# Where the hidden activations are squared, copied and split, in a three-stage attention and two-layer MLP kernel in a hand-ordered schedule

## The chip, the cores and the metric

One core of a Trainium2 chip. The kernel runs as one program on that core. The metric is the device time of one execution in microseconds (us). The median of three timed runs of the kernel before is 681.76 us (680.63 to 685.14).

## The reference, cut to what matters

Three stages follow one another. An attention over 1536 tokens (2 batches, 8 heads, head size 64) gives x of 1536 rows and 512 columns. Then come two blocks of the same shape, each with 512 inputs, 2048 hidden units and 512 outputs. They differ in the activation:

```python
h = x @ w_in
r = np.maximum(h, 0.0)
g = r * r
x = g @ w_out                      # first block

h = x @ w_in
g = np.where(h >= 1, h, np.where(h <= -1, 0.0, (h + 1) ** 2 / 4))
out = g @ w_out                    # second block
```

Inputs and outputs are fp32, the weights fp64. A matmul in one pass isn't exact enough, so each operand is held as a rounded high part and a low part (the rest), and three products (high with high, low with high, high with low) are summed.

## The kernel before, in words

The order of the work is a table of words, PLAN (lines 61 to 162), that is read from left to right: each word is a step (letters), its number and, last, an engine (a for ScalarE, v for VectorE, g for GpSimd). Steps are issued in that order, and each engine runs its own instructions strictly in the order in which they were issued; semaphores hold an instruction until its inputs are there and its output buffer is free. So the table sets, for every engine, what stands behind what. TensorE (PE), VectorE (DVE), ScalarE (ACT) and GpSimd (POOL) compute; SyncE (SP) issues the loads.

Stage 1, up to about 160 us: attention (steps S, M, E, R, N, T, O), and between its steps the first quarter of the first block, in tiles of 256 tokens (H for the first layer at L276, Y for the second at L398).

Stage 2, the rest of the first block and the whole second block: the hidden units go in groups of 512, the tokens in tiles of 384 columns. The first layer of a pair of token tiles and a pair of hidden tiles is one "quad" (28 of them, q): seven products instead of eight (steps Pa to Pg, each 6 matmuls at L308), with sums of the inputs made beforehand (steps u, "tm" and "th" tiles) and sums of the products made in between:

- Ca (L315) copies one PSUM bank to another, Cc (L318) copies a bank to the SBUF tile tm[3], Vb (L321) adds that tile to a bank, Vc (L324) writes another such sum to tm[3] itself.
- So of the four hidden tiles of a quad three end in PSUM banks 4 to 7 and one in tm[3]. `q_bank` deals the banks out.

Each hidden tile ("unit") then passes five steps. ha: ReLU (L341 on ScalarE, L343 on VectorE) or, in the second block, the clamp to -1..1 (L345, always VectorE), from the bank to one of the SBUF tiles tm. hb: the square, in place in tm (L350 and L354 on ScalarE, L352 on VectorE). hc: in the second block the product with max(h, 1) (L358, VectorE). hh: the copy that rounds to the high part gh (L362). hl: the subtraction that gives the low part gl (L366), on GpSimd unless the word ends in v. So every unit's data is in SBUF from ha on, and its PSUM bank is free after ha (in the second block after hc). The second layer (Y, 12 matmuls of 384 columns in the first block, 9 of 512 in the second, L398) reads gh and gl, which lie in rings: three tiles for even token tiles, five for odd ones.

Beside this runs the weights' way from fp64 to two fp32 parts, 64 tiles of 512 columns: loads (wl), two ScalarE steps (L205, L210), three VectorE steps (L212, L214, L216), one GpSimd add (L219), then the high part (L233, L250; ScalarE or VectorE), the low part (L238, L255; GpSimd or VectorE) and sums of weight tiles (L246). Results of the second layer are added from PSUM to acc (L423, VectorE) or copied to it (L421), and split again for the next block (L427, L432). The sums of the inputs (u) are at L487, their high parts at L513 (GpSimd), their low parts at L515; two of them use an extra SBUF tile zt.

## Time and profile before

| | |
|---|---|
| median of 3 timed runs | 681.76 us |
| the profiled execution's own time | 679.23 us |
| its span, first to last instruction | 677.5 us |
| PE busy | 598.4 us (88%), 4202 matmuls |
| VectorE busy | 571.6 us (84%), 1101 instructions |
| ScalarE busy | 296.9 us (44%), 707 |
| GpSimd busy | 357.0 us (53%), 298 |
| mean granted TensorE clock | 0.967 of full speed |

Spans and busy times are of the one profiled execution. Matmuls overlap and their ends are modelled, so that the busy time of PE isn't a measure of how fast it works; the pace of its instructions in a stretch without gaps is. A line number names the line of the kernel that issued an instruction; an arrow reads "output <- inputs". Names of tiles: bank is PSUM, all others are SBUF.

### The profile page before, as it was taken

How to read it: one execution, taken by the hardware profiler on the slowest of the kernel's cores; microseconds unless marked ns; L12 is line 12 of the kernel's file. 1: busy time of each engine (PE TensorE's matmuls, PEld its weight loads, DVE VectorE, ACT ScalarE, POOL GpSimd, SP SyncE). 2: the span in 40 equal slices, each digit the busy share in tenths (PEclk: the TensorE clock that was granted, in tenths of full speed). 3: DMA queues.
4: the chain of work that ended last, by engine and by line, in shares of the span. 5: the costliest groups of instructions: out<-in, count | busy, mean ns of one | idle time of the engine just before them, and what ended most of it. 6: DMA issues, size and time to landing. Idle time of an engine off the chain costs nothing.

```text
span 677.5 us, 11174 instructions
## 1 busy us (share of the span) xinstructions
PE 598.4 (88%) x4202; PEld 536.7 (79%) x4202; DVE 571.6 (84%) x1101; ACT 296.9 (44%) x707; POOL 357.0 (53%) x298
## 2 busy tenths in 40 slices
PE   6889889888799898999888877989889998999994
PEld 3578778777689898899887876778778787889884
DVE  5988969989998978888799999997988899877462
ACT  5666756533544434724542352343443544422320
POOL 0566757576663636663656578546535455533110
PEclk8889979989899999999998999999999999999998
DMA  8666413020111111301220110111112111100004
GB/s 329 220 246 181 143 26 80 32 94 33 62 63 63 62 63 63 124 32 43 97 79 0 62 64 0 63 62 63 62 65 60 63 63 62 63 1 0 17 15 156
DMA packets 16418, 52.17 MB, mean 77 GB/s; under 512 B 2124, under 2 KB 2732, under 8 KB 16364
## 3 DMA queue, kind: packets, MB, share of 16 engines
q1 hardware_dynamic: 16364, 51.45, 22.3%
q8 instruction: 33, 0.54, 0.3%
q14 instruction: 21, 0.17, 0.1%
HBM read 47.37 MB, written 3.15 MB: 75 GB/s over the span
## 4 chain that ended last, share of the span: by engine, by line
DVE 28%; PE 17%; issue 4%; ACT 4%; POOL 2%; DMA 1%; DVEq 0%; ACTq 0%; POOLq 0%
PE bank L398 8%; PE bank L308 8%; DVE gl L366 3%; DVE tm L358 3%; DVE tm L345 3%; DVE fx L212 3%; DVE fx L216 3%; DVE acc L423 2%; DVE fx L214 2%; ACT tm L354 1%; DVE fr L246 1%; PE bank L455 1%; DVE gh L362 1%; DVE xl L432 1%; DVE bank L321 1%
## 5 line engine op out<-in xcount | busy, mean ns | idle before, releaser
L219 POOL TENSOR_TENSOR fr<-fx,fr 128x512 uint32<-128x512 uint32 x64 | 89.8, 1409 | 100.9 <-ACT fr L205 44.4
L366 POOL TENSOR_TENSOR gl<-tm,gh 128x384 fp32r<-128x384 f32 (+1 forms) x72 | 77.1, 1074 | 85.0 <-ACT gh L362 62.3
L308 PE MATMUL bank<-xh,wih 128*128 128x384 f32 x224 | 77.7, 347 | 14.4 <-DVE bank L321 5.8
L354 ACT ACTIVATE tm<-tm,bias 128x384 f32<-128x384 f32 x64 | 38.6, 614 | 103.7 <-DVE tm L345 103.6
L308 PE MATMUL bank<-xl,wih 128*128 128x384 f32 x224 | 75.9, 339 | 1.8 <-DVE xl L515 1.8
L398 PE MATMUL bank<-gh,woh 128*128 128x384 f32 (+1 forms) x288 | 70.1, 334 | 4.1 <-ACT gh L362 2.2
L308 PE MATMUL bank<-th,wih 128*128 128x384 f32 x168 | 59.6, 355 | 15.3 <-DVE tm L324 6.3
L398 PE MATMUL bank<-gl,woh 128*128 128x384 f32 (+1 forms) x288 | 67.2, 326 | 4.1 <-DVE gl L366 4.1
L398 PE MATMUL bank<-gh,wol 128*128 128x384 f32 (+1 forms) x288 | 65.7, 320 | 0.0
L210 ACT ACTIVATE fx<-raw 128x512 f32<-128x512 f32 x64 | 42.7, 670 | 50.1 <-DMA raw<-in_wd_dram 27.0
L362 ACT CAST gh<-tm 128x384 fp32r<-128x384 f32 (+1 forms) x91 | 43.8, 489 | 41.9 <-DVE tm L358 22.5
L398 PE MATMUL bank<-woh,gh 128*128 128x512 f32 x180 | 57.4, 398 | 4.8 <-DVE acc L423 4.1
L308 PE MATMUL bank<-tl,wih 128*128 128x384 f32 x168 | 57.9, 345 | 1.5 <-DVE tl L515 1.5
L308 PEld LDWEIGHTS bank<-xh,wih 128*128 128x128 f32 x224 | 42.6, 190 | 20.9 <-DVE bank L321 7.6
L366 DVE TENSOR_TENSOR gl<-tm,gh 128x384 fp32r<-128x384 f32 (+1 forms) x64 | 55.1, 866 | 4.1 <-ACT gh L362 3.7
L398 PE MATMUL bank<-woh,gl 128*128 128x512 f32 x180 | 56.6, 396 | 1.6 <-DVE gl L366 1.2
L308 PE MATMUL bank<-xh,wil 128*128 128x384 f32 x224 | 57.6, 338 | 0.0
L398 PEld LDWEIGHTS bank<-gh,woh 128*128 128x128 f32 x288 | 50.7, 196 | 7.9 <-DVE acc L423 3.2
L398 PE MATMUL bank<-wol,gh 128*128 128x512 f32 x180 | 56.9, 397 | 0.0
L216 DVE SCALAR_TENSOR_TENSOR fx<-raw,fx 128x512 uint32<-128x512 uint32 x64 | 55.6, 874 | 0.4
L398 PEld LDWEIGHTS bank<-gl,woh 128*128 128x128 f32 x288 | 50.4, 194 | 6.0 <-DVE gl L366 6.0
L423 DVE TENSOR_TENSOR acc<-bank,acc 128x384 f32<-128x384 f32 (+1 forms) x81 | 47.2, 602 | 8.7 <-PE bank L398 8.6
(139 smaller groups left out, 1534.1 us busy)
## 6 DMA issues: line engine op xcount, KB each, us to landing
raw<-in_wd_dram SPq DMA_DIRECT2D x64, 512.0 KB
k<-in_kd_dram SPq DMA_DIRECT2D x8, 400.0 KB
out_dram<-acc SPq DMA_DIRECT2D x11, 256.0 KB
q<-in_qd_dram SPq DMA_DIRECT2D x5, 512.0 KB
vw<-in_vw_dram SPq DMA_DIRECT2D x3, 768.0 KB
vw<-in_vw_dram SPq DMA_DIRECT2D x2, 1024.0 KB
acc<-in_vb_dram SPq DMA_DIRECT2D x2, 768.0 KB
acc<-in_vw_dram SPq DMA_DIRECT2D x1, 1024.0 KB
```

Of the source, the lines that this page charges most:

```text
L210: A.activation(f32(x), f32(hi), AF.Abs)
L212: V.tensor_scalar(f32(x), f32(x), E_LOW, E_HIGH, ALU.max, ALU.min)
L216: V.scalar_tensor_tensor(x, hi, 0xC0000000, x, ALU.bitwise_and, ALU.bitwise_or)
L219: G.tensor_tensor(fr[n % 2], fx[n % 2], fr[n % 2], ALU.add)
L308: PE.matmul(q_bank(q, role), a, b, start=bool(first and i == 0), stop=i == 5, skip_group_check=not first)
L345: V.tensor_scalar(a, h, -1.0, 1.0, ALU.max, ALU.min)
L354: A.activation(a, a, AF.Square, bias=bias[:, 0:1], scale=0.5)
L358: V.scalar_tensor_tensor(a, h, 1.0, a, ALU.max, ALU.mult)
L362: cp(e)(hi, a)
L366: e.tensor_tensor(lo, a, f32(hi), ALU.subtract)
L398: PE.matmul(ys[j], a, b, start=f == 0 and i == 0 and (n >= 24 or j % 2 == 0), stop=f == GF - 1 and i == 2 and (n >= 24 or j % 2 == 1))
L423: V.tensor_tensor(a, y_bank(g, t, j), a, ALU.add)
```

## The change

- The activations no longer go through tm where PSUM will do. In the first block ReLU, square, high part and low part all work on the PSUM bank itself (for the 256-column units from the 12th on, too). In the second block the product with max(h, 1) is written back to the bank, and high and low part are made from there.
- The subtraction of the low part is thereby VectorE's, except for 7 units of the first quarter that still stand in tm.
- The clamp is two ReLUs on ScalarE, relu(2 - relu(1 - h)), in 62 of 64 units (2 stay VectorE's). The square is ScalarE's everywhere.
- The sum that went to tm[3] (Vc) goes to the bank of the quad's first unit. tm has three tiles instead of four.
- The ring for odd token tiles has six tiles instead of five; zt is gone, and tm[0] takes its place. The banks of the quads are dealt out from one bank further on.
- The high parts of the input sums (u with letters d, i, m, q) are ScalarE's or VectorE's instead of GpSimd's.
- The whole PLAN is written anew: 61 to 162 before, one line fewer after. The line numbers after are 2 to 9 higher.

The number of TensorE's instructions is the same, 2809 rows in either order. GpSimd has 208 rows instead of 301, ScalarE 699 instead of 541, VectorE 1098 instead of 1099.

```diff
--- before.py
+++ after.py
 PLAN = """
...
-hb115 Y110 da60 hc115 Vc23 dq63 ha117 hh115a saa15g hb117 Y111 wo60g ya84 sab15g dr63 hl115v Pg23 ha116 hc117 hb116
-Pa24 ya85 dq62 ha118 Y112 hc116 hh116a hb118 hl116g hc118 Pc24 hh117v sac15g ha119 Y113 ya86 sad15g hb119 Cc24v Ca24a
+hc115 dt60 hh115a dl60 ya84 Pf23 wl62 hh116v da60 wl63 hl116 Pe23 ha117a hl115 wo61g ya85 Y112 saa15g ya86 wh60a hb117
+Vc23 sab15g hc117 dq62 wo60v hh117a Pg23 ha118a hl117 sac15g Pa24 sad15g Y113 Ca24a hb118 ha119a hc118 hh118v Pb24
...
@@ -187,10 +186,13 @@
         wol = [mp.tile([128, 2 * 512], F32R, name=f"wol{i}") for i in range(2)]
         gh = [mp.tile([128, TB], F32R, name=f"gh{i}") for i in range(3)]
         gl = [mp.tile([128, TB], F32R, name=f"gl{i}") for i in range(3)]
-        tm = [mp.tile([128, TB], F32, name=f"tm{i}") for i in range(4)]
+        tm = [mp.tile([128, TB], F32, name=f"tm{i}") for i in range(3)]
         bias = mp.tile([128, 64], F32, name="bias")
         V.memset(bias[:, 0:1], 0.5)
-        th, tl, zt = [], [], []
+        V.memset(bias[:, 1:2], 1.0)
+        V.memset(bias[:, 2:3], 2.0)
+        clamped = set()
+        th, tl = [], []
 
 
 
@@ -263,7 +265,9 @@
             return bank[2 * (t == 1) + j // 2][:, j % 2 * CH:(j % 2 + 1) * CH]
 
         def h_bank(n):
-            return bank[4][:, n % 2 * CH:(n % 2 + 1) * CH] if n < 12 else bank[4 - n % 2][:, :CH]
+            if n < 12:
+                return bank[4][:, n % 2 * CH:(n % 2 + 1) * CH]
+            return bank[4 - n % 2][:, n // 2 % 2 * CH:(n // 2 % 2 + 1) * CH]
 
         def h_mm(n):
             t, f = U[n]
@@ -282,7 +286,7 @@
             return g // NG, g % NG, g, r // 2, 2 * g + r % 2
 
         def q_bank(q, role):
-            return bank[4 + (role + 3 * q) % 4][:, :TB]
+            return bank[4 + (role + 3 * q + 1) % 4][:, :TB]
 
         def x_op(tp, name, kk):
             t0, t1 = (slice((2 * tp + i) * TB, (2 * tp + i + 1) * TB) for i in (0, 1))
@@ -315,25 +319,26 @@
             cp(e)(q_bank(q, 2), q_bank(q, 0))
 
         def q_p5(q, e=A):
-            cp(e)(tm[3], q_bank(q, 1))
+            cp(e)(tm[2], q_bank(q, 1))
 
         def q_u4(q):
-            V.tensor_tensor(q_bank(q, 1), q_bank(q, 2), tm[3], ALU.add)
+            V.tensor_tensor(q_bank(q, 1), q_bank(q, 2), tm[2], ALU.add)
 
         def q_c22(q):
-            V.tensor_tensor(tm[3], q_bank(q, 2), tm[3], ALU.add)
+            V.tensor_tensor(q_bank(q, 0), q_bank(q, 2), tm[2], ALU.add)
 
         def act(n):
 
             if n < 24:
-                return h_bank(n), tm[n % 4][:, :CH], gh[n % 3][:, :CH], gl[n % 3][:, :CH], 0
+                h = h_bank(n)
+                return h, tm[n % 2][:, :CH] if n < 12 else h, gh[n % 3][:, :CH], gl[n % 3][:, :CH], 0
             q, r = divmod(n - 24, 4)
-            h = tm[3] if r == 2 else q_bank(q, (0, 1, None, 2)[r])
+            h, m = q_bank(q, (0, 1, 0, 2)[r]), quad(q)[0]
             i = g_of(q, r // 2, (0, 1, 1, 0)[r])
-            return h, tm[(0, 1, 2, 0)[r]], gh[i], gl[i], quad(q)[0]
+            return h, tm[n % 2] if m else h, gh[i], gl[i], m
 
         def g_of(q, f, t):
-            return (2 * q + f) % 3 if t == 0 else 3 + (2 * q + f) % 5
+            return (2 * q + f) % 3 if t == 0 else 3 + (2 * q + f) % 6
 
         def h_act(n, e=A):
             h, a, hi, lo, m = act(n)
@@ -341,29 +346,33 @@
                 A.activation(a, h, AF.Relu)
             elif m == 0:
                 V.tensor_scalar_max(a, h, 0.0)
+            elif e is A:
+                A.activation(a, h, AF.Relu, bias=bias[:, 1:2], scale=-1.0)
+                A.activation(a, a, AF.Relu, bias=bias[:, 2:3], scale=-1.0)
             else:
                 V.tensor_scalar(a, h, -1.0, 1.0, ALU.max, ALU.min)
-
-        def h_sq(n, e=A):
+                clamped.add(n)
+
+        def h_sq(n):
             h, a, hi, lo, m = act(n)
-            if m == 0 and e is A:
+            if m == 0:
                 A.activation(a, a, AF.Square)
-            elif m == 0:
-                e.tensor_tensor(a, a, a, ALU.mult)
+            elif n in clamped:
+                A.activation(a, a, AF.Square, bias=bias[:, 0:1], scale=0.5)
             else:
-                A.activation(a, a, AF.Square, bias=bias[:, 0:1], scale=0.5)
+                A.activation(a, a, AF.Square, scale=0.5)
 
         def h_mul(n):
             h, a, hi, lo, m = act(n)
-            V.scalar_tensor_tensor(a, h, 1.0, a, ALU.max, ALU.mult)
+            V.scalar_tensor_tensor(h, h, 1.0, a, ALU.max, ALU.mult)
 
         def h_hi(n, e=V):
             h, a, hi, lo, m = act(n)
-            cp(e)(hi, a)
-
-        def h_lo(n, e=G):
+            cp(e)(hi, h if m else a)
+
+        def h_lo(n, e=V):
             h, a, hi, lo, m = act(n)
-            e.tensor_tensor(lo, a, f32(hi), ALU.subtract)
+            e.tensor_tensor(lo, h if m else a, f32(hi), ALU.subtract)
 
 
 
@@ -473,7 +482,7 @@
             t0, t1 = (slice((2 * tp + i) * TB, (2 * tp + i + 1) * TB) for i in (0, 1))
             z = acj[:, 0:2, 1024:1024 + TB], acj[:, 2:4, 1024:1024 + TB]
             if n in (1, 2):
-                z = (zt[0].unsqueeze(1),) * 2
+                z = (tm[0].unsqueeze(1),) * 2
             return tp, k, k2, t0, t1, z
 
         def t_step(n, c, e):
@@ -702,10 +711,10 @@
             lp = late.enter_context(tc.tile_pool(name="late_s", bufs=1, side="right"))
             for l, name in ((th, "th"), (tl, "tl")):
                 l.append(lp.tile([128, 3, 2, TB], F32R, name=f"{name}1"))
-            for i in range(3, 8):
+            for i in range(3, 9):
                 gh.append(lp.tile([128, TB], F32R, name=f"gh{i}"))
                 gl.append(lp.tile([128, TB], F32R, name=f"gl{i}"))
-            zt.append(lp.tile([128, TB + 88], F32, name="zt")[:, :TB])
+            lp.tile([128, 24], F32, name="pad")
 
         step = {"kl": k_load, "ql": q_load, "qf": q_first, "cl": c_load, "nl": vn_load, "bl": vb_load, "vl": v_load, "vf": vs_fill,
                 "wl": w_load, "km": k_sum, "S": s_mm, "M": s_max,
@@ -718,7 +727,7 @@
         step.update({f"d{c}": partial(w_high, k=k) for k, c in enumerate("qrst")})
         step.update({f"sa{c}": partial(lambda n, e=G, k=0: w_sum(n, k, e), k=k) for k, c in enumerate("abcd")})
         step.update({c: partial(q_mm, what=c) for c in PRODUCTS})
-        step.update({f"u{c}": partial(lambda n, e=G, c="": t_step(n, c, e), c=c) for c in "abcdefghijklmnopqr"})
+        step.update({f"u{c}": partial(lambda n, e, c: t_step(n, c, e), c=c, e=A if c in "dimq" else G) for c in "abcdefghijklmnopqr"})
         eng = {"a": A, "v": V, "g": G}
         for word in PLAN.split():
             name, n, e = re.fullmatch(r"([A-Za-z]+)(\d+)([avg]?)", word).groups()
```

Three places show how instructions move. The first is VectorE around the last sum of quad 20 (L324 before, L328 after), in the second block; fx, fr, woh and wol are weights, acc is the result. Before:

```order
L324 TENSOR_TENSOR tm_97<-bank_69,tm_97 128x384
L238 TENSOR_TENSOR wol_87<-fr_78,woh_85 128x512
L423 TENSOR_TENSOR acc<-bank_63,acc 128x512
L345 TENSOR_SCALAR tm_95<-bank_68 128x384
L212 TENSOR_SCALAR fx_77<-fx_77 128x512
L212 TENSOR_SCALAR fx_76<-fx_76 128x512
L214 TENSOR_SCALAR fx_77<-fx_77 128x512
L214 TENSOR_SCALAR fx_76<-fx_76 128x512
L345 TENSOR_SCALAR tm_96<-tm_97 128x384
L216 SCALAR_TENSOR_TENSOR fx_77<-raw_75,fx_77 128x512
L358 SCALAR_TENSOR_TENSOR tm_96<-tm_97,tm_96 128x384
L233 CAST wih_1562<-fx_77 128x256
```

After:

```order
L328 TENSOR_TENSOR bank_68<-bank_70,tm_96 128x384
L432 TENSOR_TENSOR acc<-bank_63,acc 128x512
L235 CAST woh_85<-fx_76 128x512
L367 SCALAR_TENSOR_TENSOR bank_68<-bank_68,tm_94 128x384
L367 SCALAR_TENSOR_TENSOR bank_69<-bank_69,tm_95 128x384
L235 CAST woh_85<-fx_77 128x512
L375 TENSOR_TENSOR gl_1932<-bank_68,gh_1931 128x384
L375 TENSOR_TENSOR gl_1930<-bank_69,gh_1929 128x384
L240 TENSOR_TENSOR wol_87<-fr_78,woh_85 128x512
L214 TENSOR_SCALAR fx_76<-fx_76 128x512
L367 SCALAR_TENSOR_TENSOR bank_70<-bank_70,tm_95 128x384
L216 TENSOR_SCALAR fx_76<-fx_76 128x512
```

The clamps (L345) are gone, the products (L358, now L367) write the bank they read, and the low parts (L375) stand on VectorE with the bank as first input; and the next steps on the weights (L212, L214 before, L214, L216 after) come behind the products and low parts of two units instead of between the clamps.

The second place is ScalarE at the units of the same quad; raw and fr are weights. Before:

```order
L354 ACTIVATE tm_94<-tm_94,bias 128x384
L233 CAST woh_85<-fx_76 128x512
L210 ACTIVATE fx_76<-raw_74 128x512
L233 CAST woh_85<-fx_77 128x512
L210 ACTIVATE fx_77<-raw_75 128x512
L354 ACTIVATE tm_95<-tm_95,bias 128x384
L362 CAST gh_89<-tm_94 128x384
L354 ACTIVATE tm_96<-tm_96,bias 128x384
```

After:

```order
L350 ACTIVATE tm_94<-bank_68,bias 128x384
L351 ACTIVATE tm_94<-tm_94,bias 128x384
L363 ACTIVATE tm_94<-tm_94 128x384
L207 ACTIVATE fr_78<-raw_74 128x512
L350 ACTIVATE tm_95<-bank_69,bias 128x384
L351 ACTIVATE tm_95<-tm_95,bias 128x384
L350 ACTIVATE tm_94<-bank_68,bias 128x384
L351 ACTIVATE tm_94<-tm_94,bias 128x384
L363 ACTIVATE tm_94<-tm_94 128x384
L212 ACTIVATE fx_76<-raw_74 128x512
L363 ACTIVATE tm_95<-tm_95 128x384
```

Where one square (L354) stood per unit, there are now two ReLUs and a square (L350, L351, L363) per unit, one behind the other on the same tile.

The third place is GpSimd where it adds the weight tiles 52 to 57 (L219 before, L221 after), at the same place in the program. Before:

```order
L219 TENSOR_TENSOR fr_78<-fx_76,fr_78 128x512
L219 TENSOR_TENSOR fr_79<-fx_77,fr_79 128x512
L366 TENSOR_TENSOR gl_1932<-tm_95,gh_1931 128x384
L366 TENSOR_TENSOR gl_92<-tm_94,gh_89 128x384
L238 TENSOR_TENSOR wol_87<-fr_79,woh_85 128x512
L219 TENSOR_TENSOR fr_79<-fx_77,fr_79 128x512
L366 TENSOR_TENSOR gl_1926<-tm_95,gh_1925 128x384
L366 TENSOR_TENSOR gl_93<-tm_94,gh_90 128x384
L366 TENSOR_TENSOR gl_1928<-tm_96,gh_1927 128x384
L219 TENSOR_TENSOR fr_78<-fx_76,fr_78 128x512
L366 TENSOR_TENSOR gl_91<-tm_94,gh_88 128x384
```

After:

```order
L221 TENSOR_TENSOR fr_78<-fx_76,fr_78 128x512
L221 TENSOR_TENSOR fr_79<-fx_77,fr_79 128x512
L240 TENSOR_TENSOR wol_87<-fr_79,woh_85 128x512
L221 TENSOR_TENSOR fr_79<-fx_77,fr_79 128x512
L221 TENSOR_TENSOR fr_78<-fx_76,fr_78 128x512
L248 TENSOR_TENSOR fr_79<-fr_79 128x256
L240 TENSOR_TENSOR wil_1606<-fr_78,wih_1605 128x512
L248 TENSOR_TENSOR fr_79<-fr_78,fr_79 128x256
L248 TENSOR_TENSOR fr_78<-fr_79,fr_78 128x256
```

The low parts of the activations (L366) are gone from this queue; only work on the weights is left in it.

## Rows read from the trace of the kernel before

**Rows 1.** stretches of the span: busy time of each engine (instructions), clock, DMA; last their sum
```profile
160.00:420.00 260.00, 227.62 (x1229) 215.44 (x1227) 231.86 (x358) 109.86 (x218) 150.80 (x123) 0.97 0.17 58
420.00:600.00 180.00, 166.23 (x794) 143.06 (x795) 160.60 (x266) 74.02 (x136) 95.76 (x81) 0.99 0.17 59
600.00:660.00 60.00, 60.00 (x295) 52.87 (x295) 38.64 (x71) 18.53 (x36) 13.38 (x12) 1.00 0.03 10
...
sum 678.00, PE 598.42 PEld 536.73 DVE 571.60 ACT 296.92 POOL 357.00; mean PE 99.74 PEld 89.46 DVE 95.27 ACT 49.49 POOL 59.50
```

**Rows 2.** chain that ended last: start us, us, what, matmuls merged
```profile
648.15 4.18 PE bank L308 x24
652.34 8.21 PE bank L398 x36
...
296.58 5.55 PE bank L398 x32
```

**Rows 3.** the same stretches, quad matmuls of L308 alone: PE and PEld busy (count)
```profile
160.00:420.00 260.00, 116.01 (x589) 104.87 (x588) 0.97 0.17 58
420.00:600.00 180.00, 84.87 (x434) 76.64 (x435) 0.99 0.17 59
```

**Rows 4.** the same stretches, second-layer matmuls of L398 alone
```profile
160.00:420.00 260.00, 121.63 (x640) 111.42 (x639) 0.97 0.17 58
420.00:600.00 180.00, 90.28 (x360) 66.82 (x360) 0.99 0.17 59
```

**Rows 5.** waits of PE, 160 to 600 us: total us, times, longest
```profile
PE bank L308 <- DVE bank L321: 10.1, 8, 2.4
```

**Rows 6.** timeline of VectorE near 405 us: start us, us, what
```profile
404.67 0.55 DVE L366 TENSOR_TENSOR gl<-tm,gh 128x384 fp32r<-128x384 f32 x1
405.14 0.55 DVE L358 SCALAR_TENSOR_TENSOR tm<-bank,tm 128x384 f32<-128x384 f32 x1
...
410.63 2.21 DVE L366 TENSOR_TENSOR gl<-tm,gh 128x384 fp32r<-128x384 f32 x1
```

**Rows 7.** timeline of GpSimd in the same stretch, releaser in brackets
```profile
404.83 0.98 POOL L246 TENSOR_TENSOR fr<-fr,fr 128x256 f32<-128x256 f32 x1 [0.36 <-DVE fr L246]
...
410.58 1.85 POOL L487 TENSOR_TENSOR acc<-acc 128x768 f32<-128x768 f32 x1 [1.69 <-DVE acc L487]
```

**Rows 8.** single lines of VectorE: count, duration ns min/median/max, first and last start
```profile
L366 DVE TENSOR_TENSOR gl<-tm,gh x64: 407/614/2215, 79.2 to 660.2; 128x384 fp32r<-128x384 f32 x55, 128x256 fp32r<-128x256 f32 x9
...
L212 DVE TENSOR_SCALAR fx<-fx x64: 397/427/2061, 18.0 to 595.2; 128x512 f32<-128x512 f32 x64
...
L423 DVE TENSOR_TENSOR acc<-bank,acc x81: 537/551/692, 199.4 to 661.3; 128x384 f32<-128x384 f32 x48, 128x512 f32<-128x512 f32 x33
...
L343 DVE TENSOR_SCALAR tm<-tm x5: 343/346/1441, 207.0 to 309.7; 128x384 f32<-128x384 f32 x5
```

**Rows 9.** groups by line and form: count, busy us, mean ns, idle before
```profile
L366 POOL TENSOR_TENSOR gl<-tm,gh 128x384 fp32r<-128x384 f32 x57 | 63.9, 1126 | 73.8 <-ACT gh L362 55.7 <-DVE gh L362 18.1
...
L366 DVE TENSOR_TENSOR gl<-tm,gh 128x384 fp32r<-128x384 f32 x55 | 46.9, 856 | 4.1 <-ACT gh L362 3.7
...
L212 DVE TENSOR_SCALAR fx<-fx 128x512 f32<-128x512 f32 x64 | 45.8, 720 | 7.1 <-ACT fx L210 6.9
...
L354 ACT ACTIVATE tm<-tm,bias 128x384 f32<-128x384 f32 x64 | 38.6, 614 | 103.7 <-DVE tm L345 103.6
L362 ACT CAST gh<-tm 128x384 fp32r<-128x384 f32 x75 | 37.5, 508 | 36.7 <-DVE tm L358 22.5 <-DVE tm L352 11.0 <-PE bank L398 2.9
...
L345 DVE TENSOR_SCALAR tm<-bank 128x384 f32<-128x384 f32 x48 | 26.1, 549 | 8.7 <-PE bank L308 5.8 <-POOL gl L366 2.4
...
L362 DVE CAST gh<-tm 128x384 fp32r<-128x384 f32 x37 | 20.1, 547 | 0.3
...
L352 DVE TENSOR_TENSOR tm<-tm 128x384 f32<-128x384 f32 x20 | 18.6, 930 | 5.9 <-ACT tm L341 5.9
...
L341 ACT ACTIVATE tm<-bank 128x384 f32<-128x384 f32 x22 | 10.7, 489 | 32.6 <-PE bank L308 19.6 <-DVE gl L366 7.0 <-POOL gl L366 6.1
```

More of the change, by code (lines that the diff above doesn't have):

```diff
@@ L162 @@
+Cc27a hb132 Vb27 hc132 hh132a Pe27 hl132 ya98 Pf27 Vc27 Pg27 ha133a Y127 ha134a ya100 hb134 ya101 hb133 Y128 ya102
+hc133 ha135a hh133v Y129 hb135 hc135 hh135a Y130 hl135 hc134 hh134a Y131 ya104 hl134 ya106 hl133 Z0 Z3 Z1 za3 ya105 Z2
+za1 za0 zd1 yd105 yd101 yd96 zd3 yd104 yd100 yd98 yd102 yd106 yd97 za2 zd2 zd0
 """
```

192 lines of the change are left out of this document (94 added, 98 removed).

## The prediction

> **What bounds the kernel now.** I read the stretches of the span first, then the pace of PE, then single instructions of VectorE.
>
> The stretches [rows 1] show two kinds of time. From 600 to 660 us PE is busy for all 60 us, and VectorE for 38.6. From 160 to 600 us (440 us, two thirds of the run) VectorE is busy for 231.9 + 160.6 = 392.5 us, 89%, while PE's busy time has holes. How large the holes are is read from PE's own pace, since its busy time is modelled. Where nothing holds it [rows 2], a quad matmul takes 4.18 / 24 = 0.174 us, a second-layer matmul of 384 columns 5.55 / 32 = 0.173 and one of 512 columns 8.21 / 36 = 0.228. With the counts of the stretches [rows 3, 4]: 160 to 420 us needs 589 x 0.174 + 640 x 0.173 = 213 us of PE (a tenth of those 640 have another width; I leave that), and 420 to 600 us needs 434 x 0.174 + 360 x 0.228 = 158. That is 371 of 440 us, so 69 us are lost to PE there. The longest of its waits is for VectorE's L321 [rows 5], and VectorE is the engine that is nearly always busy. So the bound is VectorE's queue, with PE 69 us behind it as the next floor.
>
> What fills VectorE? Not only its own work. The low part L366 takes 0.55 us at 404.67 and 2.21 us at 410.63 [rows 6], the same form both times. At 410.58 GpSimd starts an instruction of 1.85 us [rows 7], and VectorE's instruction ends only after it. In contrast an instruction with one input in PSUM (L358 at 405.14) takes its 0.55 us while GpSimd works from 404.83 to 405.81. The ranges say the same [rows 8]: forms that read only SBUF go from 397 to 2061 ns (L212) and to 2215 ns (L366), while L423, which reads PSUM, stays between 537 and 692 over both its sizes. So an instruction of VectorE that reads SBUF alone can be blocked by GpSimd for up to 1.7 us, and one that reads PSUM isn't seen to be.
>
> **The change part by part**, as VectorE's time over the whole run (571.6 us busy [rows 1]). An unblocked 384-column instruction of VectorE with a PSUM input is taken at 0.55 us, after L345's 549 ns [rows 9].
>
> Clamps: 64 before, 48 from PSUM at 0.549 and 16 from tm at 0.346 or more (the form of L343 [rows 8]); two stay. 46 x 0.549 + 16 x 0.346 = 31 us leave. On ScalarE each becomes two ReLUs, which the trace doesn't show with a bias from PSUM; I take 489 (L341, from a bank) and 614 ns (L354, with a bias) [rows 9], at least twice 489 and at most twice 614, so 62 x 1.10 = 68 us more. ScalarE is at 297 us [rows 1] and goes to about 370 to 390 of some 640; beside VectorE's load that is cover enough, if its queue is in the right order.
> ScalarE: Activation LUTs, section Rules for kernel authors, in the Trainium skill says to use VectorE and not ScalarE for relu, max and min. The trace agrees on the price of one step (1.10 us against 0.55). By that rule the 31 us would be no gain and the sum below -12 us instead of -43; by the rows they are one, as ScalarE's 297 us and VectorE's 572 [rows 1] leave the room on ScalarE.
>
> Squares: 20 x 0.930 us leave [rows 9]; 12 smaller ones of 256 columns are estimated at 0.7 each. 27 us leave. ScalarE takes them in 0.5 us each, 16 us.
>
> Low parts: before 55 x 0.856 = 47 us [rows 9] and 9 small ones at about 0.9, 55 us. After, the order has 112 of 384 columns from PSUM at 0.55, 12 small ones from PSUM at about 0.42 and 5 small ones from tm at 0.9: 71 us. So 16 us more, though VectorE does 65 more of them: the unblocked price pays for most of GpSimd's share.
>
> High parts: before 37 x 0.547 [rows 9] and 8 small ones, 25 us; after 49 x 0.55 from PSUM, 5 x 0.42 and 2 small ones, 30 us: 5 more. Unblocked they were cheaper from SBUF (346 ns, as L343 [rows 8]) than 0.55 from PSUM; what they gain is that they are not blocked.
>
> Other moves by count of the order: 8 more copies between banks (4.4 us), about ten more low parts of weights and four fewer sums (6), nine more steps on the input sums net (9), fewer casts and evictions (-5); the 16 products that read tm read PSUM now, which I value at -5, an estimate. Sum +9.
>
> VectorE directly: -31 - 27 + 16 + 5 + 9 = -28 us.
>
> What stays exposed: the three weight steps. L212 averages 720 ns where 397 is its least [rows 8, 9]: 64 x 0.32 = 21 us of blocking, and the two steps that follow are taken to be alike, 62 in all. GpSimd loses 57 x 1.126 = 64 us [rows 9] and some 7 of small low parts, so it goes from 357 to about 286 us, and lower by the casts that leave it: 0.75 of before. If blocking falls in that ratio, 15 us go; none if GpSimd's rest still stands beside the same steps; some 45 if the new order keeps the two apart. I take 15, since the rows can't tell where they will meet.
>
> Sum for VectorE: -43 us, between -28 and -73.
>
> From there to the time. Nearly all of it lies in 160 to 600 us (4 or so before), so VectorE needs 392.5 - 39 = 353 us there. At the share it reaches now as the bound, 89%, the stretch takes 353 / 0.89 = 397 us, 43 less than 440. PE would then be at 371 / 397 = 93% of its pace, more than the 158 / 180 = 88% of its better stretch and less than the 99% after 600 us. That is consistent, so no new bound needs to come before it. After 600 us nothing is to be had. Before 160 us I count nothing: the gains there are a few us, and ScalarE gets work. The profiled execution (679.2 us) would take 636; the median of the runs shown is 2.5 us above it, so 638 us.
>
> **The rivals.**
>
> PE becomes the bound. If the new order keeps GpSimd off VectorE, VectorE loses 73 us, needs 320 in the stretch and has slack; then PE at 99% of its pace sets 371 / 0.99 = 375, 65 us less: 617 us. For it: the stretch after 600 us, where VectorE at 64% lets PE run full. Against: the order doesn't show when things meet.
>
> VectorE stays crowded: blocking only moves to the weights' steps, and waits for ScalarE (two ReLUs, square, high part) open holes in VectorE's own queue. Half the gain remains, 662 us. For it: before, 103.6 us of ScalarE's idle time ahead of L354 ended with VectorE's clamp [rows 9], so these engines hand work to and fro; now the hand-over goes ScalarE, VectorE, ScalarE, VectorE for each unit.
>
> ScalarE's chain is what counts. Each of 62 clamps takes 1.10 instead of 0.55 us on the way from bank to gh; if all of it showed, 34 us would come back: 672 us. Against: the units of a quad overlap. This is the outcome to which the rule named above points.
>
> The slower side: banks are held. Before, a unit's bank was free after the clamp and the product; now it is held until the low part is made, which is 0.49 + 0.61 + 0.61 + 0.55 + 0.51 + 0.55 = 3.3 us of work (L341, L354 twice, L345, L362, L345 [rows 9]) behind the last product, plus the queues, and the quad's first bank is used again for the fourth sum. PE's first product into that bank in the next quad must wait for it. A quad has 42 x 0.174 + 48 x 0.173 = 15.6 us of PE, so there is room if units are done promptly. If the low part stands late in VectorE's queue, each quad loses time: above 43 / 28 = 1.5 us per quad the whole gain is gone, and at 2 us it is 28 x 2 - 43 = 13 us slower: 695 us. Against: the order puts product, high part and low part of a unit near each other on VectorE.
>
> **How the numbers follow.** A measurement here tells a difference of about 1% (6.8 us) from none. The forecast, 638 us, gets 0.61, PE as the bound 0.13, half the gain 0.13, ScalarE's chain 0.05, held banks 0.08. The first three are faster: 0.87. ScalarE's 672 us lies by the edge of 1% (675), so its 0.05 stands for no change; held banks are slower, 0.08. The range leaves out held banks, ScalarE's chain, and the ends of the first cases: 614 to 664 us.
>
> **What would show it.** Right: L375 (the low part) on VectorE at 0.55 us with a narrow spread; L214's mean nearer to 0.4 than 0.72 us; GpSimd's busy time near 270 us, ScalarE's near 380, VectorE's near 530; PE's pace in the middle of the run above 90%. Wrong: blocking of the weight steps as before or more; PE waits at L308's counterpart for VectorE's low part (banks held); VectorE idle for ScalarE's square or high part for tens of us. The forecast is wrong as a whole if VectorE's busy time falls by 40 us and the span doesn't: then VectorE wasn't the bound, but the chain through the engines.

## The result and the profile after

The changed kernel takes 596.18 us (median of 4 runs, 594.4 to 598.26) against 682.45 us for the kernel before in the same comparison: a ratio of 0.873, 95% interval 0.868 to 0.878. The forecast was 638 us with a range of 614 to 664. The direction was right, but the gain is 86 us where 44 were forecast, and the time lies below the range.

From the page of the profiled execution after (594.42 us): the span, the busy times, and the shares of the chain that ended last, by engine.

```profile
span 592.6 us, 11185 instructions
...
PE 569.6 (96%) x4202; PEld 527.9 (89%) x4202; DVE 474.7 (80%) x1097; ACT 373.9 (63%) x866; POOL 243.5 (41%) x207
...
PE 84%; DVE 6%; DMA 5%; ACT 2%; issue 1%; SPq 0%; ACTq 0%; DVEq 0%
```

PE is at 96% (88% before) and VectorE at 80% with 97 us less busy time than before (571.6 [rows 1] to 474.7). 84% of the chain is PE. The stretches after, with columns as in [rows 1], and here from 60 us on:

```profile
60.00:160.00 100.00, 99.92 (x1193) 95.56 (x1192) 87.73 (x244) 73.22 (x215) 58.43 (x48) 1.00 0.28 87
160.00:420.00 260.00, 259.36 (x1431) 250.01 (x1430) 219.49 (x434) 164.10 (x325) 121.28 (x100) 1.00 0.20 73
420.00:580.00 160.00, 160.00 (x796) 143.19 (x795) 116.92 (x221) 94.00 (x178) 38.24 (x34) 1.00 0.10 37
sum 580.00, PE 567.49 PEld 526.07 DVE 473.03 ACT 373.91 POOL 243.47; mean PE 141.87 PEld 131.52 DVE 118.26 ACT 93.48 POOL 60.87
```

From 60 to 580 us PE is busy for 519.3 of 520 us at a granted clock of 1.00. VectorE is still busy for 84% of the stretch 160 to 420 and for 73% of 420 to 580, so it is no longer what PE waits for. The same early stretch of the kernel before:

```profile
60.00:160.00 100.00, 88.47 (x1076) 81.15 (x1076) 88.93 (x218) 57.20 (x186) 69.45 (x58) 0.95 0.24 71
```

Here too the gap is gone: 88.5 us of PE busy before, 99.9 after, and 117 more matmuls in this stretch.

Waits of PE over the whole span after (total us, times, longest). The three largest belong to the attention; the last one shown answers to [rows 5].

```profile
PE bank L602 <- DVE ks L590: 3.0, 3, 1.5
PE bank L643 <- DVE vw L675: 2.9, 1, 2.9
PE bank L602 <- DVE sm L610: 1.8, 2, 1.2
...
PE bank L312 <- DVE bank L325: 0.5, 2, 0.3
```

The 10.1 us for VectorE's sum (L321, now L325) are 0.5. A wait of the first layer (L312) for a low part (L375), the sign of held banks, isn't among the rows.

Groups by line and form after, which answer to [rows 9] (count, busy us, mean ns, idle before):

```profile
L221 POOL TENSOR_TENSOR fr<-fx,fr 128x512 uint32<-128x512 uint32 x64 | 84.6, 1333 | 152.6 <-DVE fx L218 82.9 <-ACT fr L207 51.0 <-DVE bank L367 6.1
...
L375 DVE TENSOR_TENSOR gl<-bank,gh 128x384 fp32r<-128x384 f32 x112 | 60.9, 551 | 12.0 <-ACT gh L371 11.1
...
L218 DVE SCALAR_TENSOR_TENSOR fx<-raw,fx 128x512 uint32<-128x512 uint32 x64 | 44.7, 706 | 0.4
...
L351 ACT ACTIVATE tm<-tm,bias 128x384 f32<-128x384 f32 x62 | 38.3, 618 | 2.0
...
L350 ACT ACTIVATE tm<-bank,bias 128x384 f32<-128x384 f32 x62 | 35.9, 579 | 50.7 <-PE bank L312 41.2 <-DVE bank L328 7.0 <-DVE bank L367 2.5
L367 DVE SCALAR_TENSOR_TENSOR bank<-bank,tm 128x384 f32<-128x384 f32 x64 | 35.5, 561 | 23.1 <-ACT tm L363 23.0
...
L363 ACT ACTIVATE tm<-tm 128x384 f32<-128x384 f32 x62 | 32.1, 522 | 0.9
...
L216 DVE TENSOR_SCALAR fx<-fx 128x512 uint32<-128x512 uint32 x64 | 31.1, 488 | 0.4
...
L214 DVE TENSOR_SCALAR fx<-fx 128x512 f32<-128x512 f32 x64 | 30.3, 481 | 7.7 <-ACT fx L212 7.5
...
L371 DVE CAST gh<-bank 128x384 fp32r<-128x384 f32 x49 | 26.7, 551 | 4.9 <-ACT bank L359 4.3 <-PE bank L407 0.2
```

The low part (L375) on VectorE costs 551 ns in place of 856 and of GpSimd's 1126. The three weight steps L214, L216 and L218 (L212, L214, L216 before) take 30.3 + 31.1 + 44.7 = 106.1 us; before, the same 192 instructions take 45.8 [rows 9] + 43.1 + 55.6 = 144.5:

```profile
L216 DVE SCALAR_TENSOR_TENSOR fx<-raw,fx 128x512 uint32<-128x512 uint32 x64 | 55.6, 874 | 0.4
...
L214 DVE TENSOR_SCALAR fx<-fx 128x512 uint32<-128x512 uint32 x64 | 43.1, 678 | 0.5
```

L214's mean is 481 ns where L212's was 720. One line of VectorE after, to be held against [rows 8] (count, ns min/median/max):

```profile
L375 DVE TENSOR_TENSOR gl<-bank,gh x124: 407/548/560, 108.0 to 574.5; 128x384 fp32r<-128x384 f32 x112, 128x256 fp32r<-128x256 f32 x12
```

The low part's longest is 560 ns: none of the 124 is blocked. In the kernel before the same step, reading tm, went up to 2215 ns.

To sum the blocking, I add up for each form of VectorE its count times (mean minus least duration). That is 156 us before and 44 after. That GpSimd is behind it shows in the same trace: of VectorE's instructions before, 196 run more than 100 ns over the least of their form, and every one of them overlaps an instruction of GpSimd; forms that read a bank have 5 of the 156 us. So 112 us of blocking went, more than the 97 us by which VectorE's busy time fell. The unblocked part of VectorE's busy time has risen by some 15 us.

Where PE's time came from can be counted too: for each matmul, the part of its distance to the one before, from start to start, that exceeds 1.15 times the median of its form. That sum is 59.0 us before 160 us of the span and 65.8 behind it in the kernel before; after, it is 41.8 and 3.3. So 17.2 us came from the first 160 us and 62.5 from the rest; the other 5 of the 85 us by which the span fell (677.5 to 592.6) lie below that threshold.

### The profile page after: what moved, and what is told of

It is laid out like the page before. It is cut to its first block, busy times and chain, and to the rows that moved or that the text cites. A ratio compares the mean times of both kernels' runs of the same rounds, so it can differ in the third digit from the quotient of the medians.

```text
span 592.6 us, 11185 instructions
## 1 busy us (share of the span) xinstructions
PE 569.6 (96%) x4202; PEld 527.9 (89%) x4202; DVE 474.7 (80%) x1097; ACT 373.9 (63%) x866; POOL 243.5 (41%) x207
## 4 chain that ended last, share of the span: by engine, by line
PE 84%; DVE 6%; DMA 5%; ACT 2%; issue 1%; SPq 0%; ACTq 0%; DVEq 0%
PE bank L407 40%; PE bank L312 31%; PE bank L280 5%; PE bank L602 3%; DMA raw<-in_wd_dram 2%; PE bank L632 2%; PE bank L643 2%; DMA k<-in_kd_dram 2%; PE bank L464 1%; DMA q<-in_qd_dram 1%; DVE fx L214 1%; DVE ks L590 1%; DVE fx L218 1%; DVE s L610 1%; ACT fr L207 1%
## 5 line engine op out<-in xcount | busy, mean ns | idle before, releaser
L221 POOL TENSOR_TENSOR fr<-fx,fr 128x512 uint32<-128x512 uint32 x64 | 84.6, 1333 | 152.6 <-DVE fx L218 82.9
L375 DVE TENSOR_TENSOR gl<-bank,gh 128x384 fp32r<-128x384 f32 (+1 forms) x124 | 65.8, 538 | 14.2 <-ACT gh L371 12.9
L312 PE MATMUL bank<-xh,wih 128*128 128x384 f32 x224 | 75.8, 339 | 0.5 <-DVE bank L325 0.5
L312 PE MATMUL bank<-xl,wih 128*128 128x384 f32 x224 | 75.2, 336 | 0.0
L350 ACT ACTIVATE tm<-bank,bias 128x384 f32<-128x384 f32 x62 | 35.9, 579 | 50.7 <-PE bank L312 41.2
L407 PE MATMUL bank<-gh,woh 128*128 128x384 f32 (+1 forms) x288 | 66.2, 321 | 0.0
L407 PE MATMUL bank<-gl,woh 128*128 128x384 f32 (+1 forms) x288 | 65.1, 317 | 0.0
L212 ACT ACTIVATE fx<-raw 128x512 f32<-128x512 f32 x64 | 42.5, 670 | 25.3 <-DMA raw<-in_wd_dram 19.5
L312 PE MATMUL bank<-xh,wil 128*128 128x384 f32 x224 | 57.1, 335 | 0.0
L312 PE MATMUL bank<-th,wih 128*128 128x384 f32 x168 | 56.3, 335 | 0.2 <-DVE bank L319 0.2
L312 PE MATMUL bank<-tl,wih 128*128 128x384 f32 x168 | 56.4, 336 | 0.0
L367 DVE SCALAR_TENSOR_TENSOR bank<-bank,tm 128x384 f32<-128x384 f32 x64 | 35.5, 561 | 23.1 <-ACT tm L363 23.0
L407 PEld LDWEIGHTS bank<-gh,wol 128*128 128x128 f32 x288 | 49.0, 189 | 0.0
L207 ACT ACTIVATE fr<-raw 128x512 uint32<-128x512 uint32 x64 | 42.3, 668 | 5.8 <-DVE fx L216 2.1
L218 DVE SCALAR_TENSOR_TENSOR fx<-raw,fx 128x512 uint32<-128x512 uint32 x64 | 44.7, 706 | 0.4
```

Of the source, the lines that this page charges most:

```text
L207: A.activation(fr[n % 2], w_raw(n, 0), AF.Copy, scale=2.0 ** -29)
L212: A.activation(f32(x), f32(hi), AF.Abs)
L218: V.scalar_tensor_tensor(x, hi, 0xC0000000, x, ALU.bitwise_and, ALU.bitwise_or)
L221: G.tensor_tensor(fr[n % 2], fx[n % 2], fr[n % 2], ALU.add)
L312: PE.matmul(q_bank(q, role), a, b, start=bool(first and i == 0), stop=i == 5, skip_group_check=not first)
L350: A.activation(a, h, AF.Relu, bias=bias[:, 1:2], scale=-1.0)
```

## The experiments

Two questions were to be told apart: which part of the change brings the gain (the new order, the new division of work between engines, PSUM as the source, fewer GpSimd instructions, the sixth ring tile), and through what (less load on VectorE, or banks that come free in time). All runs, against the kernel before on the same chip:

| run | what it is | median us | ratio, 95% interval |
|---|---|---|---|
| (after) | the whole change | 596.18 | 0.868 to 0.878 |
| order_alone | new order, old division of work | 663.88 | 0.968 to 0.978 |
| mix_alone_2 | new division of work, old order | 777.14 | 1.134 to 1.145 |
| ring_of_five | five ring tiles | 595.63 | 0.871 to 0.877 |
| units_in_sbuf | products, high and low parts through SBUF | 626.28 | 0.915 to 0.923 |
| low_parts_on_gpsimd | the same, 57 low parts on GpSimd | 626.32 | 0.916 to 0.921 |
| gpsimd_load | 57 added GpSimd instructions | 611.12 | 0.893 to 0.898 |
| clamps_on_vector | clamps on VectorE | 606.17 | 0.886 to 0.891 |
| late_low | low parts stand later in the order | 620.71 | 0.903 to 0.917 |
| tight_banks_3 | 13 steps of TensorE moved | 621.56 | 0.904 to 0.913 |

**order_alone.** The changed kernel's order with the old division of work: hidden units from 24 on go through SBUF tiles, clamps on VectorE, 20 squares back on VectorE, low parts on the engines they had. Five tm tiles and five ring tiles. Not all of the old division is back: the small units 12 to 23 still work in PSUM, and the sum Vc still goes to a bank.

```diff
-            return h, tm[n % 2] if m else h, gh[i], gl[i], m
+            return h, tm[(0, 1, 3, 4)[n % 4]] if m else tm[(1, 3, 4)[n % 3]], gh[i], gl[i], m
...
-            V.scalar_tensor_tensor(h, h, 1.0, a, ALU.max, ALU.mult)
+            V.scalar_tensor_tensor(a, h, 1.0, a, ALU.max, ALU.mult)
...
-            e.tensor_tensor(lo, h if m else a, f32(hi), ALU.subtract)
+            e.tensor_tensor(lo, a, f32(hi), ALU.subtract)
```

> The new order with the old division of work: the units from the 24th on are squared, copied and split in SBUF tiles, clamps on VectorE, 32 squares tried on VectorE, the low parts on the engine that had them before (57 of the large ones on GpSimd), ring of five. Theory 1 (what VectorE reads decides: instructions that read SBUF alone get blocked wherever they stand): blocking returns, VectorE's busy time goes back to some 550 us and the time to 650 to 680 us. Theory 2 (the order decides: it keeps SBUF work of VectorE off GpSimd): most of the gain stays, 610 to 630 us.

Measured: 663.88 us, 18 us less than before. VectorE's groups and two of PE's waits in that run:

```profile
L218 DVE SCALAR_TENSOR_TENSOR fx<-raw,fx 128x512 uint32<-128x512 uint32 x64 | 50.1, 790 | 0.5
L377 DVE TENSOR_TENSOR gl<-tm,gh 128x384 fp32r<-128x384 f32 x55 | 41.6, 761 | 5.1 <-ACT gh L373 4.8
L214 DVE TENSOR_SCALAR fx<-fx 128x512 f32<-128x512 f32 x64 | 38.4, 608 | 5.8 <-ACT fx L212 5.7
...
L216 DVE TENSOR_SCALAR fx<-fx 128x512 uint32<-128x512 uint32 x64 | 34.6, 543 | 0.4
```

```profile
PE bank L312 <- DVE bank L325: 12.6, 7, 3.2
PE bank L409 <- DVE gl L377: 9.6, 5, 2.7
```

The order, with what stays of the new division, brings about a fifth of the gain. The time lies in the first theory's range, but the blocking doesn't return as a whole: it is 109 us against 156. L214 takes 608 ns where L212 took 720, the low part from tm 761 where it took 856. But PE waits for VectorE as it did before (12.6 us for the sum, 9.6 for low parts).

**mix_alone, mix_alone_2.** The new division of work with the old order, and five ring tiles; what the new buffers need earlier is pulled forward (258 of 2277 steps). In mix_alone one product of quad 2 stood ahead of the sum that it adds to, so that quad's values were other ones; mix_alone_2 has it in place.

```diff
-            return bank[4 + (role + 3 * q + 1) % 4][:, :TB]
+            return bank[4 + (role + 3 * q) % 4][:, :TB]
...
-            return h, tm[n % 2] if m else h, gh[i], gl[i], m
+            return h, tm[(0, 1, 3)[n % 3]] if m else h, gh[i], gl[i], m
...
-            return (2 * q + f) % 3 if t == 0 else 3 + (2 * q + f) % 6
+            return (2 * q + f) % 3 if t == 0 else 3 + (2 * q + f) % 5
```

> The new division of work (units in PSUM, low parts on VectorE, clamps as two ReLUs on ScalarE) in the old order, where steps are pulled forward only as far as the banks and tiles ask (257 of 2277). Theory 1: most of the gain stays, since the blocked instructions are gone: 610 to 630 us, the three weight steps on VectorE still at about 600 ns for L214. Theory 2: the old order lets GpSimd and VectorE meet as before and the banks are held long: 650 to 680 us.

> The new division of work in the old order again, with one more step (a product of quad 2) pulled forward so that every sum reads what it should. After mix_alone: the held banks decide, 770 to 785 us, with PE waiting some 70 us for VectorE's low part. If that waiting came from the misplaced product, below 720 us.

Measured: 777.86 and 777.14 us, 95 us slower than before and outside the ranges of both theories of mix_alone. The busy times and PE's waits of mix_alone_2:

```profile
PE 632.6 (82%) x4202; PEld 569.0 (74%) x4202; DVE 508.6 (66%) x1097; ACT 377.3 (49%) x866; POOL 243.6 (32%) x207
```

```profile
PE bank L310 <- DVE gl L373: 72.0, 31, 5.7
PE bank L310 <- DVE bank L326: 12.1, 7, 4.2
PE bank L405 <- DVE acc L430: 9.6, 5, 5.2
```

VectorE has less work than before (508.6 against 571.6 us) and is idle for a third of the span, and yet the time is longer. TensorE's first layer waits 72 us, 31 times, for the low part (L373) that sets a bank free: the held banks of the fourth rival. So a smaller load on VectorE isn't enough: the new division pays only in the new order (-18 us for the order alone, +95 for the division alone, -86 together).

**ring_of_five.** The ring for odd token tiles back at five.

```diff
-            return (2 * q + f) % 3 if t == 0 else 3 + (2 * q + f) % 6
+            return (2 * q + f) % 3 if t == 0 else 3 + (2 * q + f) % 5
...
-            for i in range(3, 9):
+            for i in range(3, 8):
```

> Only the ring for odd token tiles goes back from six to five tiles. Both theories: no more than 1% slower (596 to 602 us), since the order leaves every tile free in time with five as well. If the sixth tile is what uncouples PE from VectorE, over 610 us. It is also the control for the runs that use the two tiles this frees.

Measured: 595.63 us, with an interval inside that of the whole change. The sixth tile neither costs nor gains anything that shows here.

**units_in_sbuf.** Order and engines of the changed kernel; the three lines of order_alone's diff, so that high and low part are made from SBUF and banks are free after the product. Five ring tiles.

> Order and engines as in the changed kernel, ring of five, but the units from the 24th on go through SBUF tiles: ReLU or clamp from the bank to the tile, square, product, high and low part from there. So 112 low parts and 49 high parts of VectorE read SBUF alone instead of PSUM. Theory 1: they get blocked by GpSimd (41% busy) and lengthen from 0.55 to some 0.75 us, about 25 us more on VectorE, which has 118 us of slack: 600 to 615 us. If PSUM as the place matters for more than that (bank hold, hand-over), the time moves the other way, below 596.

Measured: 626.28 us, 30 us over the whole change and above the 615 that the first theory allowed. The low part now reads tm (count, ns min/median/max):

```profile
L375 DVE TENSOR_TENSOR gl<-tm,gh x117: 395/559/2091, 61.5 to 604.0; 128x384 fp32r<-128x384 f32 x112, 128x256 fp32r<-128x256 f32 x5
```

Its mean over the 112 of 384 columns is 824 ns instead of 551, 30 us more, its longest 2091 instead of 560. VectorE's busy time is 507.1 us, and blocking 89 us instead of 44. All of this increase lies in the units' own low and high parts (48 us instead of 2); the three weight steps are blocked for 11.7 us, not more than the 14.3 of the changed kernel. PSUM as the place of the units is worth these 30 us, though the banks are held longer for it.

**gpsimd_load.** The changed kernel with five ring tiles and, for 57 units, an added GpSimd subtraction of 384 columns between spare tiles whose result nothing reads.

```diff
+            if n in EXTRA:
+                G.tensor_tensor(tm[4], tm[3], tm[3], ALU.subtract)
```

> The changed kernel with ring of five and, at 57 of the low parts, one more GpSimd subtraction of 128x384 between two spare SBUF tiles that nobody reads: GpSimd's busy time as before the change (243 + 57 x 1.05 = 303 us), nothing else moved. Theory 1 (VectorE's SBUF steps meet GpSimd): L214 and L216 lengthen from 0.48 to some 0.6 us, GpSimd's real work comes later; 600 to 612 us. Theory 2 (the order alone keeps the two apart): under 600 us and the weight steps unchanged.

Measured: 611.12 us, 15 us more. GpSimd is busy for 294.6 us instead of 243.5. VectorE's low part and two of its weight steps (L215 and L217 are L214 and L216 of after):

```profile
L378 DVE TENSOR_TENSOR gl<-bank,gh 128x384 fp32r<-128x384 f32 x112 | 60.8, 550 | 10.8 <-ACT gh L372 10.0
...
L215 DVE TENSOR_SCALAR fx<-fx 128x512 f32<-128x512 f32 x64 | 36.9, 585 | 7.4 <-ACT fx L213 7.4
...
L217 DVE TENSOR_SCALAR fx<-fx 128x512 uint32<-128x512 uint32 x64 | 33.3, 523 | 0.4
```

The low part from PSUM stays at 550 ns beside the busier GpSimd, while the weight steps go from 481 and 488 to 585 and 523. Blocking rises from 44 to 62 us, that of the weight steps from 14.3 to 25.8. So in one run the steps that read SBUF alone lengthen beside GpSimd and the one that reads PSUM doesn't. How much of the 15 us is this blocking and how much GpSimd's own later work wasn't separated.
The Trainium skill (SBUF — State Buffer, section Who interferes with whom) says that a VectorE instruction with at most one SBUF input, outside its two-port modes, doesn't contend with GpSimd; the longest of the 124 low parts, 558 ns in this run, agrees.

**low_parts_on_gpsimd.** units_in_sbuf with the low parts of the same 57 units on GpSimd.

> units_in_sbuf with 57 of the low parts on GpSimd as before the change: VectorE loses 57 x 0.82 = 47 us, GpSimd gains 57 x 1.13 = 64. Theory 1 (blocking follows GpSimd's load, and a low part on GpSimd takes twice as long and comes later): 630 to 650 us, slower than units_in_sbuf's 626. If only VectorE's sum counted, 605 to 620 us.

Measured: 626.32 us, the same as units_in_sbuf, where 630 to 650 were expected. VectorE's busy time falls by 14 us alone (507.1 to 493.1), though its low parts of 384 columns fall by 43 (91.3 to 48.5): with GpSimd at 311.7 us the blocking of its other steps rises from 58 to 81 us. With SBUF as the source it made no difference to the time whose the low part was.

This run and order_alone have the same order, the same places in SBUF and nearly the same low parts on GpSimd, and it is 38 us faster. What differs is the engines of other steps: clamps and 20 squares on ScalarE, the high parts of the input sums off GpSimd, and some of the weights' steps. They weren't tried one by one in this setting.

**clamps_on_vector.** The changed kernel with all clamps as VectorE's one instruction instead of ScalarE's two ReLUs.

```diff
-hl116 Pe23 ha117a hl115 wo61g
+hl116 Pe23 ha117v hl115 wo61g
```

> Only the 62 clamps go back to VectorE, one instruction from the bank instead of two ReLUs. VectorE gets 62 x 0.55 = 34 us more (to some 508 us), ScalarE 74 us less, and a unit's way from bank to low part is 0.65 us shorter. Theory 1 (VectorE has slack now, PE is the bound): 596 to 606 us. Theory 3 (VectorE's load still counts, by its share as in my forecast): 34 us x 0.7 or more, 615 to 630 us. If ScalarE's chain was what counted, below 594.

Measured: 606.17 us, 10 us more, at the upper edge of the first theory. Busy times:

```profile
PE 575.9 (95%) x4202; PEld 528.2 (87%) x4202; DVE 506.5 (84%) x1159; ACT 310.6 (51%) x742; POOL 244.4 (40%) x207
```

VectorE's 62 added instructions put 32 us on it (474.7 to 506.5) and 63 come off ScalarE (373.9 to 310.6). A third of VectorE's increase shows in the time: with PE at 95% VectorE has slack, but not everywhere.

**late_low.** The changed kernel with the low parts of the units from 24 on standing up to 25 words later, as far as their readers and the bank's next user allow. A piece of the order (hl115 stands further on, behind sac15g):

```diff
-hl116 Pe23 ha117a hl115 wo61g ya85 Y112 saa15g ya86 wh60a hb117
+Pe23 ha117a wo61g ya85 Y112 saa15g ya86 wh60a hb117 hl116
```

> The changed kernel with its division of work and its order, but the low parts of the units from 24 on are written up to 25 words later in PLAN, as far as their readers and the next user of their bank allow (5.6 words later in the mean). The number of instructions of each engine is that of the changed kernel. Theory A (it counts how soon a bank is free): with a span of some 593 us for 2277 words a word is worth about 0.26 us, so a unit is finished some 1 to 2 us later; waits of TensorE for the low part come up by 10 us or more, and the time is 603 to 630 us. Theory B (only VectorE's load counts, and it has slack): 592 to 600 us, the waits of TensorE stay under 5 us.

Measured: 620.71 us, 25 us more, with the same instructions on every engine; VectorE's busy time is 483.3 us, 9 more. Of PE's waits:

```profile
PE bank L310 <- DVE gl L373: 13.6, 18, 2.5
```

This wait isn't there in the changed kernel. From a unit's last product to the end of its low part the mean over 112 units is 8.6 us, against 7.0 in the changed kernel, 8.4 in mix_alone_2 and 13.4 in the kernel before (whose banks didn't wait for it). A mean delay of 1.6 us per unit goes with 25 us of time.

**tight_banks, tight_banks_2, tight_banks_3.** The changed kernel with some second-layer steps behind a next product of the coming quad instead of ahead of it, so that TensorE has less to do between a unit's last product and the next product into its bank. In the first two some of the moved steps came behind the step that writes the next weights over theirs, so they read other weights; the third keeps all steps ahead of it. One of the 13 moved steps:

```diff
-Pa24 sad15g Y113 Ca24a hb118 ha119a hc118 hh118v Pb24
+Pa24 sad15g Ca24a hb118 ha119a hc118 hh118v Pb24 Y113
```

> The changed kernel with 18 of the second-layer steps (Y, from 24 on) moved behind the next quad's first products, so that TensorE has less other work queued between a unit's last product and the next product into its bank: under 6 us of it in 10 of 54 places instead of 1, as the old order has in 17. Engines, instructions and all other words are as in the changed kernel. Theory A (room in TensorE's queue before a bank is used again is what the new order brings): low parts come about 7 us behind the last product, so each of these ten places waits for one to three us, 600 to 620 us, with waits at L312 for VectorE's L375 and L325. Theory B (where the other engines' instructions stand decides): 592 to 600 us.

> As tight_banks, with the moved second-layer steps kept ahead of the steps that write their inputs' tiles anew (the ring has six tiles; the first version reckoned with five): 19 steps moved, under 6 us of other TensorE work in 12 of 54 places. Theory A (room before a bank is used again): 612 to 630 us, with 8 us or more of waits of TensorE's first layer for VectorE's low part. Theory B (the 27 us of tight_banks came from steps that stood in a wrong place): 592 to 602 us.

> The changed kernel with 13 of the second-layer steps (Y26, Y48, Y50, Y66, Y74, Y81, Y97, Y98, Y108, Y109, Y113, Y124, Y125) moved behind a next product of the coming quad; all steps still read the weights and hidden tiles that they should (the two versions before moved 18 and 19, a few of them past the cast that writes the weight tile anew). Under 6 us of other TensorE work between a unit's last product and the next product into its bank in 9 of 54 places instead of 1. Theory A (room before a bank is used again): waits of TensorE's first layer for VectorE's low part of 5 us or more, 604 to 620 us. Theory B (the misplaced reads caused the 27 and 30 us): 593 to 600 us.

Measured: 623.65 and 626.22 us, and 621.56 for the third, 25 us more than the whole change and just above the 604 to 620 of its first theory. PE's waits in the third:

```profile
PE bank L310 <- DVE gl L373: 9.7, 7, 2.8
PE bank L310 <- ACT bank L317: 4.9, 3, 3.8
```

The low parts are as prompt as before (7.1 us against 7.0), so nothing on VectorE is late; TensorE comes for the bank too early. The copy L317 shares in it: it fills a bank that a unit held, waits for that unit's low part (9.3 us of ScalarE's idle time, in 8 places), and a product waits for the copy. In the changed kernel the copy (L319 there) waits for low parts too, 8.5 us, but PE waits for it for 0.2 us alone. The time lost exceeds the waits named (9.7 and 4.9 us); where more goes is seen in four neighbouring stretches of this run:

```profile
500.00:505.00 5.00, 5.00 (x28) 4.59 (x26) 2.66 (x5) 1.93 (x4) 0.99 (x1) 1.00 0.15 61
505.00:510.00 5.00, 1.18 (x5) 1.13 (x5) 4.59 (x9) 4.14 (x9) 0.99 (x1) 0.76 0.31 105
510.00:515.00 5.00, 5.00 (x15) 4.17 (x15) 2.46 (x4) 0.28 (x1) 2.99 (x3) 0.56 0.00 0
515.00:520.00 5.00, 5.00 (x27) 4.44 (x26) 0.76 (x2) 1.98 (x4) 0.00 (x0) 1.00 0.01 3
```

In 505 to 510 us PE does 5 matmuls. In the next 5 us the granted clock is 0.56, and PE does 15 matmuls instead of the 27 or 28 of its neighbours (most of the 15 have 512 columns), though it is busy throughout. The timeline of ScalarE's copy and of PE at that place (start us, us, what, idle before and what ended it):

```profile
508.35 0.46 ACT L317 COPY bank<-bank 128x384 f32<-128x384 f32 x1 [0.27 <-DVE gl L373]
...
508.87 0.69 PE L310 MATMUL bank<-th,wih 128*128 128x384 f32 x1 [3.82 <-ACT bank L317]
509.35 0.53 PE L310 MATMUL bank<-tl,wih 128*128 128x384 f32 x1
509.67 0.53 PE L310 MATMUL bank<-th,wih 128*128 128x384 f32 x1
509.99 0.53 PE L310 MATMUL bank<-tl,wih 128*128 128x384 f32 x1
```

The copy starts when the low part (L373) is done, and the product when the copy is. Behind the wait of 3.82 us the matmuls start 0.32 us apart, about twice the 0.174 of [rows 2].

## Why the prediction was right and wrong

**What bounds the kernel: right.** VectorE's queue held PE up, and behind it PE's own pace was the next floor. (PE's wait for L321 [rows 5] is the largest in total, 10.1 us, not the longest: one for L423 took 3.9.) With VectorE relieved PE runs nearly without gaps from 60 us on.

**VectorE's own terms: nearly right.** Busy time by step, before to after: clamps -34 us (forecast -31), squares -28 (-27), low parts +13 (+16), high parts +5 (+5). L375 takes 0.551 us (0.55), a clamp by two ReLUs 0.579 + 0.618 = 1.20 (1.10). The prices of a square and of a ReLU from a bank come from these rows of before:

```profile
L352 DVE TENSOR_TENSOR tm<-tm 128x384 f32<-128x384 f32 x20 | 18.6, 930 | 5.9 <-ACT tm L341 5.9
...
L341 ACT ACTIVATE tm<-bank 128x384 f32<-128x384 f32 x22 | 10.7, 489 | 32.6 <-PE bank L308 19.6 <-DVE gl L366 7.0 <-POOL gl L366 6.1
```

**"What stays exposed": the term that was mis-sized.** The three weight steps were to lose 15 us of blocking and lost 38 (144.5 to 106.1 us busy), near the stated end of 45. The rest ("other moves", +9) came out at -15. Together the sum was -97 us, where the prediction had -43 and -73 as its far end.

Counted as above, the weight steps' blocking was 52.4 us (the prediction took 62) and is 14.3. The prediction scaled it by GpSimd's busy time (0.75, near 270 us; measured 0.68, 243.5 of 357.0) and put the order at nothing, "since the rows can't tell where they will meet". The runs show both parts: with the new order and GpSimd at 344.0 us (order_alone) it is 31.3 us, with the old order and GpSimd at 243.6 (mix_alone_2) 30.3. So the lighter GpSimd takes 17 to 22 us, about what the rule gave, and the order 16 to 21 more, for which the prediction had nothing. (mix_alone_2 is also spread over a longer span, which may make its figure lower.) Which of the moves in the order does it wasn't tried.

The blocking of the units' own steps (clamps, squares, high and low parts) falls from 48 to 2 us; that is the work by PSUM and by ScalarE, which the prediction had in its own terms. All other steps of VectorE fell from 56 to 28 us, where the prediction had counted 5 (the 16 products); that is most of the difference between -15 and +9.

**"At the share it reaches now as the bound, 89%": the step that failed as a method.** It turned VectorE's gain into time as if VectorE stayed the bound. With 97 us less it doesn't: its share is 84% in 160 to 420 us and 73% in 420 to 580, and PE sets the time. That is the first rival, which I gave 0.13 and 617 us. Its cause came about as told (GpSimd kept off VectorE, 97 us where it asked for 73).

**"Before 160 us I count nothing": wrong by 17 us.** PE lost 59.0 us in that stretch before and 41.8 after. The first rival's 617 less these 17.2 is 599.8, against 596.18 measured. The reason for counting nothing was that ScalarE gets work there. It does (94.5 to 115.8 us up to 160 us), but it isn't what PE waited for.

**The rivals.** ScalarE's chain didn't decide. VectorE does wait for ScalarE more than before (23.0 us ahead of L367, where it was 10.2 ahead of L358), but PE hardly waits for VectorE any more. clamps_on_vector is 10 us slower.
The Trainium skill's rule (ScalarE: Activation LUTs, section Rules for kernel authors) to use VectorE for relu, max and min would have lost these 10 us here. A clamp is dearer on ScalarE (1.20 us for two instructions against 0.55 for one), but ScalarE had the room.

Held banks didn't come in the changed kernel, though the mechanism is real: 72.0 us of it in mix_alone_2. The price point given, 1.5 us per quad, is passed there: from the first to the last matmul of the 28 quads a quad takes 21.6 us there, against PE's own 15.6 (before, 18.6; after, 15.6). "The order puts product, high part and low part of a unit near each other on VectorE" was the argument against it, and that is half of it. late_low shows that half. tight_banks_3 shows the other, which the prediction didn't see: how much other work TensorE has queued before it comes back to a bank. Counted from the order by the paces of [rows 2], under 6 us of it lie there at 1 of 54 places in the new order, at 9 in tight_banks_3 and at 17 in the order of mix_alone_2, where a unit's low part comes 8.4 us behind its last product.

**The range.** Half of the forecast gain would be 660 us, where the rival has 662; that changes nothing. The range left the first rival's 617 inside, but had both mis-sized terms on the same side. An upper end for the gain should have been worked out from PE's floor over the whole span rather than from one stretch.

**Where the lost time goes.** The named waits explain only part of what late_low, tight_banks_3 and units_in_sbuf lose. The traces allow a sum: PE's idle time, and what its busy time loses at the lower clock (busy time times one less the granted clock). Against the changed kernel the span grows by 29.2, 26.9 and 29.6 us; the idle time takes 17.5, 16.6 and 20.5 of it, the clock 4.6, 7.5 and 2.2, and 3 to 7 us are in neither. In mix_alone_2 against before, the idle time is 60 us more and the clock costs 39 more. Of the 85 us by which the span fell with the change itself, 56 are idle time and 13 the clock.

What stays open: which of the moved steps keeps VectorE and GpSimd apart, and how the 38 us between order_alone and low_parts_on_gpsimd divide among the engine choices.
